# Layer A's output product in paired chunks, and streamed weights released by steps of TensorE

## The chip, the cores and the metric

The kernel runs on one core of a Trainium2 chip, as one launch. A core has TensorE (matrix products; its weight loads are shown apart as PEld), VectorE (DVE), ScalarE (ACT), GpSimd (POOL) and SyncE (SP), each with its own instruction stream, and 16 DMA engines that all of them share. The metric is device time of the launch in microseconds; lower is better. Each kernel is run several times and the median counts. A profiled execution comes beside the runs, and all durations here are from it.

## The reference

Four layers, A B A B, each added to the residual stream of 2048 rows of 640 numbers (bf16). Layer B is linear attention with a softmax feature map, and the change doesn't touch it. Layer A is a recurrence over 64 segments of 32 rows: 8 memory rows and the segment's 32 rows go through attention with 32 heads of 192, and the first 8 output rows are the next segment's memory.

```python
for s in range(n_seg):                                  # 64 segments
    xs = x[:, s * seg_len:(s + 1) * seg_len, :]
    h = jnp.concatenate([mem, xs], axis=1)              # 8 + 32 rows of 640
    q = jnp.einsum('btd,dhe->bhte', h, Wq)              # 32 heads x 192
    k = jnp.einsum('btd,dhe->bhte', h, Wk)
    v = jnp.einsum('btd,dhe->bhte', h, Wv)
    scores = jnp.einsum('bhqe,bhke->bhqk', q, k) * scale
    p = _softmax(jnp.where(mask[None, None], scores, -1e9), axis=-1)
    o = jnp.einsum('bhqk,bhke->bhqe', p, v)
    o = jnp.einsum('bhte,hed->btd', o, Wo)              # the output product
    mem = o[:, :M, :]                                   # feeds the next segment
    outs.append(o[:, M:, :])
```

So a segment can't begin before the memory rows of the one before are there.

## The kernel before, in words

**Segments and rounds.** `A_pre` works out what doesn't depend on the recurrence (the last eight rows of each segment), and `A_chain` runs the 64 segments. In a segment 32 rows (8 of memory, 24 of the input) are worked on in four rounds of eight heads. `order = rounds(s)` is 0, 1, 2, 3 in even segments and 3, 2, 1, 0 in odd ones, so that the weights of the round that ended one segment are there when the next begins. The order of work on every engine is that of the program text (`manual_schedule`), SP's queue of transfers included.

**The projections.** `project(hT, ps, m, n, s, steps)` (L976 to L994) is the product of the segment's 32 rows with one round's weights of Q, K or V: five steps over the 640 inputs, each with four matmuls of 384 columns that write four groups of 32 partitions side by side. `to_raw` (ScalarE, L1001) takes Q and K out of PSUM, `to_rows` (VectorE, L1006 to L1011) turns them, and `v_rows` (ScalarE L1020, VectorE L1022) takes out V. Round n + 1's Q, K and V projections stand between the parts of round n: scores (`scores`, L1028 and L1033), exponential (`weigh`, L1103), values (`attend`, L1044 and L1051), scaling (`scaled`, L1064 and L1066), turning (`turn`, L1167 and L1174).

**The output product.** `wo_round(W, r, OT, first, last, part)` (L1082 to L1088) is one round's share of the output product. It has twelve chunks i, each a 128 x 32 block of attended values (`OT`) against 128 x 640 of output weights. The 640 outputs are spread over four groups of 32 partitions, 160 columns each: 4 matmuls a chunk, 48 a round, 192 a segment, all into one PSUM bank `W`. The round 0 part runs after Q of round 2, parts of round 1 after Q of round 3 and after the loop, round 2 around the last `attend`, and round 3 at the segment's end.

**The end of a segment.** After the last product, one matmul and one weight load keep TensorE from idling (`keep_busy`, `fill(SEG_FILL)`). VectorE turns `W` (L1235) and copies the eight memory rows into `hT` (L1236), input rows 2 to 4 first, then 0 and 1, in the order in which Q of the next segment reads them. Then come `keep_tail` (L1068 to L1075: a reciprocal on VectorE, a scaled copy `otr` on ScalarE, a transposition `otb` on VectorE), `store_tail` (a transfer on POOL's queue) and `keep_rows` (L952 to L955: four ScalarE copies of 32 x 160 out of `W`). The next segment's Q0, K0, V0 and Q1 follow on TensorE, then its first scores.

**Streamed weights.** The weights don't all fit on chip. Of each of Q, K and V, three pieces (of five) of the two end rounds 0 and 3 share slots, and so do the output weights of rounds 0 and 3 (`wo_end`). Each segment therefore loads three pieces of Q, three of V (384 KB each), three of K (in halves of 192 KB) and six of output weights (320 KB): about 5.5 MB, all on SP's queue. A slot's load (`load_slot`) is issued inside `project` of round 0, behind the matmuls that last read the slot. The output weights are issued all six at once (`load_wo`, L1183) after the round 0 product in iteration n = 1. Their readers are round 3's projections and product.

**Fillers.** `FILL` and `SEG_FILL` put single weight loads into TensorE's stream: 65 or 79 after Q0 of a layer's first segment, one at the end of each segment.

Of the kernel before, what the change touches and what calls it, by code (L numbers as in the profile page):

```python
# [117 lines left out]
class Kernel:  # L118
# [523 lines left out]
    def layer_A(self, xn_dram, at_dram, li, x_raw=None):  # L642
# [29 lines left out]
        assert at + 36 * 1280 == ARENA  # L672
        unread = set(res)

        def load_slot(m, r, b, whole=False):
            if holds.get((m, b)) != r:
                holds[m, b] = r
                w = PW if whole or m in "QV" else PW // 2
                for h in range(0, PW, w):
                    nc.sync.dma_start(out=slot[m, b][:, h:h + w], in_=wview[m][:, b, PW * r + h:PW * r + h + w])  # L680

        def load_matrix(m, r):
            for b in range(KC):
# [6 lines left out]
        early = {(0, 4), (0, 5), (2, 4), (2, 5), (1, 0), (1, 1), (1, 2), (1, 3)}  # L690

        def load_wo(r, into=None, part=range(6)):
            t = into if into is not None else wo_end[:, :] if r in (0, 3) else wo_mid[:, 7680 * (r - 1):7680 * r]
            for k in part:
                tk = t[:, 1280 * k:1280 * k + 1280]
                load = nc.sync.dma_start(out=tk, in_=self.wo_rows[r, :, 1280 * k:1280 * k + 1280])
                if r in (0, 3):
                    self.last_load = load

        def piece(m, r, b):  # L700
            assert (m, r, b) in res or holds[m, b] == r
# [217 lines left out]
    def A_chain(self, xn_dram, at_dram, li, load_slot, piece, load_wo, late_wo, wo_mid, wo_end, low):  # L919
# [3 lines left out]
        with tc.tile_pool(name=f"A{li}_ch", reuse_waits="tile", bufs=1) as sp, \  # L923
# [26 lines left out]
                return sp.tile([P, KC, 32], BF16, name="hT", tag="hT")  # L950

            def keep_rows(W):  # L952
                for g in range(4):
                    last = nc.scalar.activation(out=orow[:, 160 * g:160 * g + 160], in_=W[32 * g:32 * g + 32, 0:160], func=ACT.Copy)  # L954
                self.chain_end.append(last)  # L955

            def store_rows(s):
                nc.gpsimd.dma_start(out=at_dram[32 * s:32 * s + 24, :], in_=orow[8:32, :])
# [17 lines left out]
            def project(hT, ps, m, n, s, steps):  # L976
                order = rounds(s)
                r = order[n]
                ns = SLOTS[m]
                for i in steps:  # L980
                    b = (i + KC - ns) % KC if n == 0 else i
                    w = piece(m, r, b)
                    for g in range(4):
                        if m == "V":
                            hp = 2 * (g % 2) + g // 2
                            rhs = w[:, 384 * hp:384 * hp + 384]
                        else:
                            w3 = w[:, 32 * g:32 * g + 32]
                            rhs = ap3(w3, [list(w3.ap[0]), [P, 6], [768, 2], [1, 32]])
                        o = ps  # L990
                        nc.tensor.matmul(o[32 * g:32 * g + 32, 0:384], lhsT=hT[:, b, :], rhs=rhs, start=(i == 0),  # L991
                                         stop=(i == KC - 1), tile_position=(0, 32 * g), skip_group_check=True)
                    if n == 0 and b >= KC - ns:
                        load_slot(m, order[NR - 1], b)  # L994

            def values(hT, n, s, pv, steps):
                project(hT, pv, "V", n, s, steps)
# [26 lines left out]
            def scores():  # L1024

                S = pop.tile([P, 512], F32, name="ps_s", tag="s", bufs=2)
                m = self.mk[0:80, :]
                nc.tensor.matmul(S[0:80, 0:320], lhsT=self.ident[0:80, 0:80], rhs=ap3(m, [list(m.ap[0]), [0, 4], [1, 80]]),  # L1028
                                 start=True, stop=False, skip_group_check=True)
                for x in range(2):  # L1030
                    for i, q0, q1 in ((0, 0, 1), (1, 1, 3), (2, 3, 4)):
                        c0 = 160 * x + (80 if i == 2 else 0)
                        nc.tensor.matmul(S[0:80, c0:c0 + 80 * (q1 - q0)], lhsT=KT[:, 3 * x + i, :], rhs=QT[:, x, q0:q1, :],  # L1033
                                         start=False, stop=(x == 1 and i == 2), skip_group_check=True)
                return S

            pair = [None]

            def attend(E, n):
                O = pop.tile([P, 512], F32, name="ps_o", tag="o0")  # L1040
                V = Vs[n % 2]
                for G in range(2):
                    for h in range(4):
                        nc.tensor.matmul(O[32 * h:32 * h + 32, VH * G:VH * G + 193], lhsT=E[0:80, 80 * h + 32 * G:80 * h + 32 * G + 32],  # L1044
                                         rhs=V[0:80, VH * h:VH * h + 193], start=True, stop=True, tile_position=(0, 32 * h),
                                         skip_group_check=True)
                if n % 2 == 0:
                    pair[0] = pop.tile([P, 512], F32, name="ps_t", tag="o1")
                q, m = (48, 32) if n % 2 == 0 else (64, 16)
                for h in range(4):  # L1050
                    nc.tensor.matmul(pair[0][32 * h:32 * h + m, 0:193], lhsT=E[0:80, 80 * h + q:80 * h + q + m],  # L1051
                                     rhs=V[0:80, VH * h:VH * h + 193], start=True, stop=True, tile_position=(0, 32 * h),
                                     skip_group_check=True)
                return O

# [9 lines left out]
                else:  # L1065
                    nc.vector.tensor_scalar(out=out, in0=i, scalar1=rc[:, G:G + 1], scalar2=None, op0=ALU.mult)  # L1066

            def keep_tail():  # L1068
                rc = sp.tile([P, 1], F32, name="rct", tag="rct")
                nc.vector.reciprocal(out=rc[:], in_=pair[0][:, 192:193])  # L1070
                rows = sp.tile([P, 192], BF16, name="otr", tag="rawk")
                nc.scalar.activation(out=rows[:], in_=pair[0][:, 0:192], func=ACT.Copy, scale=rc[:])  # L1072
                otb = sp.tile([P, 192], BF16, name="otb", tag="otb")
                self.chain_end = [nc.vector.transpose(out=otb[:], in_=rows[:])]  # L1074
                return otb  # L1075

            def store_tail(otb, s, r):
# [4 lines left out]
            def wo_round(W, r, OT, first, last, part=range(12)):  # L1082
                w = low[:, 0:7680] if last_wo == r else wo_end[:, :] if r in (0, 3) else wo_mid[:, 7680 * (r - 1):7680 * r]
                for i in part:
                    for g in range(4):
                        nc.tensor.matmul(W[32 * g:32 * g + 32, 0:160], lhsT=OT[i // 6][:, i % 6 // 2, 32 * (i % 2):32 * (i % 2) + 32],  # L1086
                                         rhs=w[:, 640 * i + 160 * g:640 * i + 160 * g + 160], start=(first and i == 0),
                                         stop=(last and i == 11), tile_position=(0, 32 * g), skip_group_check=True)  # L1088

            def keep_busy(ps, w):  # L1090

# [8 lines left out]
            def weigh():  # L1100
                S = scores()
                E = sp.tile([P, 320], BF16, name="E", tag="E")
                nc.scalar.activation(out=E[0:80, 0:320], in_=S[0:80, 0:320], func=ACT.Exp, scale=scale)  # L1103
                return E

# [23 lines left out]
            for s in range(NSEG):  # L1129
# [5 lines left out]

                def q_or_k(m, n):
                    ps = pqp.tile([P, 512], F32, name="ps_qk", tag="qk")
                    project(hT, ps, m, n, s, range(KC))
                    return to_raw(ps, "rawk" if m == "K" else "raw")

                def v_banks():
# [35 lines left out]
                    load_wo(order[L], low[:, 0:7680])  # L1177
                for n in range(L):
                    raw = q_or_k("Q", n + 1)
                    if n == 1:  # L1180
                        wo_round(W, order[0], OTs[0], True, False)
                        if s < NSEG - 1:
                            load_wo(order[L])  # L1183
                        else:
                            tails = [self.fetch_tails(tb, low) for tb in range(2)]
                    elif n == 2:
                        wo_round(W, order[1], OTs[1], False, False, range(6))
                        otb = keep_tail()
                    E = weigh()
                    to_rows(raw, "Q")  # L1190
                    next_kq(s, n)
                    if n == 2:
                        store_tail(otb, s, order[1])
                    raw = q_or_k("K", n + 1)
                    O = attend(E, n)
                    tails_after(n)
                    rc = weigh_rows(O)
                    to_rows(raw, "K")
                    pv = v_banks()
                    project(hT, pv, "V", n + 1, s, range(KC))  # L1200
                    osc = sp.tile([P, 384], BF16, name="osc", tag="raw")
                    for G in range(2):
                        scaled(osc[:, 192 * G:192 * G + 192], O, rc, G, "s")
# [26 lines left out]
                keep_busy(idle, 512)  # L1230
                fill(SEG_FILL)
                if s + 1 < NSEG:
                    wt = sp.tile([P, KC, 32], F32, name="wt", tag="raw")
                    for b0, b1 in ((2, 5), (0, 2)):
                        nc.vector.transpose(out=wt[:, b0:b1, :], in_=W[:, 0:160].rearrange("p (j b) -> p b j", b=KC)[:, b0:b1, :])  # L1235
                        nc.vector.tensor_copy(out=hT[:, b0:b1, 0:8], in_=wt[:, b0:b1, 0:8])  # L1236
                store_tail(keep_tail(), s, order[L])
                keep_rows(W)
            store_rows(NSEG - 1)

    def fetch_tails(self, tb, low):
# [82 lines left out]
```

## Time and profile before

| what | value |
|---|---|
| median of 3 runs | 3756.55 us (3747.55 to 3760.22) |
| profiled execution | 3738.2 us, its span 3736.4 us |
| granted TensorE clock, mean | 0.956 |
| busy: PE, PEld, DVE, ACT, POOL | 88%, 58%, 63%, 49%, 39% |
| TensorE matmuls recorded | 70,850 |
| transferred | 929.28 MB, mean 249 GB/s |
| chain that ended last, by engine | PE 63%, DVE 11%, issue 9%, DMA 6%, ACT 6%, POOL 1% |

Times in the profile are microseconds from the span's start, unless marked ns. L1086 is line 1086 of the kernel. A group of instructions reads: line, engine, operation, what it writes and reads, shape, count, then busy time and mean ns of one, then the engine's idle time before them and what ended it. "issue" is time in which the engine waited for nothing that the profile shows. Matmuls are pipelined, so their durations overlap; what one costs is read from start to start. In tables by stretch of time, each engine has its busy us and its instructions, and then come the granted clock, the share of the 16 DMA engines' time and GB/s.

### The profile page before, as it was taken

The page shows a single profiled execution, that of the slowest core. Times are in us where ns is not written, and L with a number is a line of the kernel's source. Part 1 is how long each engine was busy: PE and PEld are TensorE (multiplying, and loading weights), DVE is VectorE, ACT ScalarE, POOL GpSimd, SP SyncE. Part 2 cuts the span into 40 slices and gives each one's busy share as a digit, 9 for nine tenths or more (in the row PEclk, how much of TensorE's full clock was granted, in tenths as well). Part 3 has the DMA queues.
Part 4 walks back from the last instruction along what each step waited for, and adds up shares of the span by engine and source line. Part 5 has one row for each costly group of instructions (what it writes and reads, how often), then busy time and mean ns, then how long its engine had stood idle before and what let it go on. Part 6 is the DMA issues. An engine that isn't in the chain of part 4 may idle for free.

```text
span 3736.4 us, 167117 instructions
## 1 busy us (share of the span) xinstructions
PE 3281.7 (88%) x70850; PEld 2159.8 (58%) x71122; DVE 2357.5 (63%) x6591; ACT 1846.2 (49%) x4481; POOL 1454.6 (39%) x3917
## 2 busy tenths in 40 slices
PE   9878888888888888899999888888888888888999
PEld 7655555555555555555377555555555555555553
DVE  5456666666676666646643666666666666666475
ACT  3244555455555555446433455545555555555463
POOL 3344444444444444431122444444444444444310
PEclk9989999899999999999999899989999999999999
DMA  8887887777787877760475787777777877777600
GB/s 319 323 285 260 280 280 274 253 270 266 271 293 271 290 281 267 258 239 9 141 275 207 275 280 275 270 259 259 263 276 270 284 265 269 276 273 273 235 4 29
DMA packets 444966, 929.28 MB, mean 249 GB/s; under 512 B 71722, under 2 KB 203450, under 8 KB 441146
## 3 DMA queue, kind: packets, MB, share of 16 engines
q1 hardware_dynamic: 382746, 821.50, 61.8%
q0 software_dynamic: 59552, 83.85, 7.2%
q8 instruction: 557, 9.13, 1.0%
q10 hardware_dynamic: 1920, 13.24, 0.9%
q14 instruction: 191, 1.56, 0.1%
HBM read 850.47 MB, written 75.69 MB: 248 GB/s over the span
## 4 chain that ended last, share of the span: by engine, by line
PE 63%; DVE 11%; issue 9%; DMA 6%; ACT 6%; POOL 1%; ACTq 0%; SPq 0%; DVEq 0%; POOLq 0%
PE ps_qk L991 20%; PE ps_w L1086 13%; PE ps_v L991 8%; PE ps_s L1033 4%; PE ps_pre L878 3%; DMA arena<-wo_rows 3%; PE ps_s L1028 2%; PE ps_o L1044 2%; ACT Vp L954 2%; PE kv L1279 2%; PE ps_pre L905 2%; ACT osc L1064 2%; DVE KT L1006 2%; ACT raw L1001 1%; DVE osc L1066 1%
## 5 line engine op out<-in xcount | busy, mean ns | idle before, releaser
L991 PE MATMUL ps_qk<-arena,hT 128*32 128x384 bf16 x20480 | 1056.2, 339 | 52.7 <-DVE hT L1236 39.2
L991 PEld LDWEIGHTS <-hT 128*32 128x32 bf16 x30720 | 782.9, 98 | 483.5 <-issue 109.3
L1001 ACT ACTIVATE raw<-ps_qk 128x384 bf16<-128x384 f32 x1024 | 491.9, 491 | 365.1 <-PE ps_qk L991 327.1
L1086 PE MATMUL ps_w<-arena,OT 128*32 128x160 bf16 x18432 | 500.0, 236 | 155.0 <-issue 146.8
L1086 PEld LDWEIGHTS <-OT 128*32 128x32 bf16 x18432 | 358.1, 97 | 285.0 <-issue 176.3
L991 PE MATMUL ps_v<-arena,hT 128*32 128x384 bf16 x10240 | 512.9, 328 | 11.2 <-DMA arena<-in_A_Wv_dram 11.1
L1064 ACT ACTIVATE osc<-ps_o,rc 128x192 bf16<-128x192 f32 x896 | 335.3, 418 | 314.6 <-DVE rc L1058 313.1
L1009 DVE STREAM_TRANSPOSE QT<-raw 128x256 bf16<-128x256 bf16 x512 | 222.6, 435 | 354.0 <-ACT raw L1001 183.2
L967 POOL COPY QT<-kqb 128x64 bf16<-128x64 bf16 x512 | 121.3, 237 | 788.6 <-PE ps_s L1033 726.7
L962 POOL DMA_DIRECT2D kqb<-kqb x512 | 291.7, 570 | 165.3 <-POOL KT L970 146.8
L1103 ACT ACTIVATE E<-ps_s 80x320 bf16<-80x320 f32 x512 | 220.7, 431 | 241.4 <-PE ps_s L1033 237.6
L1006 DVE STREAM_TRANSPOSE KT<-raw 128x384 bf16<-128x384 bf16 x512 | 296.3, 579 | 65.5 <-ACT raw L1001 55.0
L1072 ACT ACTIVATE otr<-ps_t,rct 128x192 bf16<-128x192 f32 x256 | 107.8, 421 | 436.4 <-DVE rct L1070 422.7
L1022 DVE CAST Vp<-ps_v 64x384 bf16<-64x384 f32 x512 | 286.3, 559 | 35.9 <-ACT Vp L1020 20.5
L974 POOL DMA_DIRECT2D Vp<-vb x512 | 259.9, 508 | 101.9 <-PE ps_t L1051 88.0
L1086 PE MATMUL ps_w<-arena,KT 128*32 128x160 bf16 x6144 | 175.2, 278 | 128.3 <-DVE KT L1174 125.4
L1033 PE MATMUL ps_s<-QT,KT 128*80 128x80 bf16 (+1 forms) x3072 | 233.7, 213 | 49.0 <-DVE KT L1006 41.8
L1020 ACT ACTIVATE Vp<-ps_v 64x384 bf16<-64x384 f32 x512 | 246.9, 482 | 26.4 <-PE ps_v L991 25.7
L1033 PEld LDWEIGHTS <-KT 128*80 128x80 bf16 x3072 | 199.0, 119 | 87.9 <-issue 73.8
L1078 POOL DMA_DIRECT2D otb<-otb x256 | 144.5, 565 | 248.7 <-DVE otb L1074 243.1
L1086 PEld LDWEIGHTS <-KT 128*32 128x32 bf16 x6144 | 140.5, 116 | 158.0 <-DVE KT L1174 152.8
L878 PEld LDWEIGHTS <-arena 128*128 128x128 bf16 x1920 | 189.5, 99 | 43.6 <-issue 11.5
(154 smaller groups left out, 4987.1 us busy)
## 6 DMA issues: line engine op xcount, KB each, us to landing
arena<-wo_rows SPq DMA_DIRECT2D x804, 320.0 KB, 7.5
arena<-in_A_Wq_dram SPq DMA_DIRECT2D x427, 384.0 KB, 4.7
arena<-in_A_Wv_dram SPq DMA_DIRECT2D x427, 384.0 KB, 6.3
arena<-in_A_Wk_dram SPq DMA_DIRECT2D x768, 192.0 KB, 4.3
kqb<-kqb POOLq DMA_DIRECT2D x512, 48.0 KB, 5.3
arena<-in_A_Wk_dram SPq DMA_DIRECT2D x43, 384.0 KB, 7.8
vb<-arena POOLq DMA_DIRECT2D x128, 97.0 KB, 6.1
Vp<-vb POOLq DMA_DIRECT2D x512, 24.2 KB, 5.1
```

The costliest lines, as they stand in the source:

```text
L878: nc.tensor.matmul(ps[:, T * i:T * i + T], lhsT=w[b][:, P * c:P * c + P], rhs=xBT[:, b, :], start=(b == 0), stop=(b == KC - 1))
L962: nc.gpsimd.dma_start(out=kqb[:], in_=self.kqb_d[r, :, s, :])
L974: nc.gpsimd.dma_start(out=Vs[n % 2][64:80, :], in_=self.vb_d[s, r].rearrange("g t f -> (g t) f"))
L991: nc.tensor.matmul(o[32 * g:32 * g + 32, 0:384], lhsT=hT[:, b, :], rhs=rhs, start=(i == 0), stop=(i == KC - 1), tile_position=(0, 32 * g), ...
L1001: nc.scalar.activation(out=raw[:], in_=ps[:, 0:384], func=ACT.Copy)
L1006: nc.vector.transpose(out=KT[:, :, 0:64], in_=raw[:, :].rearrange("p (c j) -> p c j", j=64))
L1009: nc.vector.transpose(out=QT[:, :, 0:4:3, 0:64], in_=rv[:, :, 0:3:2, :])
L1020: nc.scalar.activation(out=o, in_=i, func=ACT.Copy)
L1022: nc.vector.tensor_copy(out=o, in_=i)
L1033: nc.tensor.matmul(S[0:80, c0:c0 + 80 * (q1 - q0)], lhsT=KT[:, 3 * x + i, :], rhs=QT[:, x, q0:q1, :], start=False, stop=(x == 1 and i == 2 ...
L1064: nc.scalar.activation(out=out, in_=i, func=ACT.Copy, scale=rc[:, G:G + 1])
L1086: nc.tensor.matmul(W[32 * g:32 * g + 32, 0:160], lhsT=OT[i // 6][:, i % 6 // 2, 32 * (i % 2):32 * (i % 2) + 32], rhs=w[:, 640 * i + 160 * ...
```

## The change

It has two parts.

**Paired chunks.** A chunk i of the output product is now two matmuls of 320 columns instead of four of 160. Even chunks write partition groups 0 and 1, odd chunks groups 2 and 3. Each group holds two separated blocks of 160 outputs, so `W` has 320 columns instead of 160, and holds two partial sums: even chunks in partitions 0 to 63, odd ones in 64 to 127. A segment has 96 of these matmuls instead of 192, and 832 instructions on TensorE instead of 1024. The two halves are added where they are read. At the segment's end VectorE makes four transpositions instead of two, and four additions in place of two copies. In `keep_rows` two ScalarE copies of 64 x 160 bring the upper half to SBUF, and four VectorE additions make the rows. `keep_rows` now stands ahead of `keep_tail`, and `keep_tail` uses another buffer (`OTh`) at the segment's end.

**Released loads.** The three V loads and the six output-weight loads of a segment are put into a list `held`. `release(step, n)` issues the next n of them with a wait on the TensorE instruction `step` added to what they already wait for. The first V load waits for the K projection of round 1, the second for V of round 1, the third for Q of round 2; the six output pieces wait for V of round 2, Q of round 3, the third scores, K of round 3, the third `attend`, V of round 3. The order of transfers on SP's queue stays.

```diff
+        held = []
+        def release(step, n=1):
+            for f in held[:n]:
+                for load in f():
+                    tc.add_manual_dep(load.ins, step.ins.name,
+                                      mybir.DependencyInfo(mybir.DependencyClass.Sync, mybir.DependencyReason.DATA),
+                                      reason="few streamed weights under way")
+            del held[:n]
...
             def keep_rows(W):
-                for g in range(4):
-                    last = nc.scalar.activation(out=orow[:, 160 * g:160 * g + 160], in_=W[32 * g:32 * g + 32, 0:160], func=ACT.Copy)
-                self.chain_end.append(last)
+                tmp = [sp.tile([P, 160], F32, name=f"wh{a}", tag=tag) for a, tag in enumerate(("E", "rawk"))]
+                for a in range(2):
+                    last = nc.scalar.activation(out=tmp[a][64:P, :], in_=W[64:P, 160 * a:160 * a + 160], func=ACT.Copy)
+                    for g in range(2):
+                        c = 320 * a + 160 * g
+                        nc.vector.tensor_tensor(out=orow[:, c:c + 160], in0=W[32 * g:32 * g + 32, 160 * a:160 * a + 160],
+                                                in1=tmp[a][64 + 32 * g:96 + 32 * g, :], op=ALU.add)
+                self.chain_end = [last]
...
                     if n == 0 and b >= KC - ns:
-                        load_slot(m, order[NR - 1], b)
+                        if m == "V":
+                            self.held.append(lambda b=b: load_slot(m, order[NR - 1], b))
+                        else:
+                            load_slot(m, order[NR - 1], b)
...
                 for i in part:
-                    for g in range(4):
-                        nc.tensor.matmul(W[32 * g:32 * g + 32, 0:160], lhsT=OT[i // 6][:, i % 6 // 2, 32 * (i % 2):32 * (i % 2) + 32],
-                                         rhs=w[:, 640 * i + 160 * g:640 * i + 160 * g + 160], start=(first and i == 0),
-                                         stop=(last and i == 11), tile_position=(0, 32 * g), skip_group_check=True)
+                    for g in range(2):
+                        q = 32 * (2 * (i % 2) + g)
+                        rhs = w[:, 640 * i:640 * i + 640].rearrange("p (a g f) -> p a g f", a=2, g=2)[:, :, g, :]
+                        nc.tensor.matmul(W[q:q + 32, 0:320], lhsT=OT[i // 6][:, i % 6 // 2, 32 * (i % 2):32 * (i % 2) + 32],
+                                         rhs=rhs, start=(first and i < 2), stop=(last and i > 9), tile_position=(0, q),
+                                         skip_group_check=True)
...
                     raw = q_or_k("Q", n + 1)
+                    if n > 0:
+                        self.release(self.step)
                     if n == 1:
                         wo_round(W, order[0], OTs[0], True, False)
                         if s < NSEG - 1:
-                            load_wo(order[L])
+                            self.held.extend(lambda k=k: load_wo(order[L], part=[k]) for k in range(6))
...
                     E = weigh()
+                    if n == 2:
+                        self.release(self.scored)
...
                     raw = q_or_k("K", n + 1)
+                    if n != 1:
+                        self.release(self.step)
                     O = attend(E, n)
+                    if n == 2:
+                        self.release(self.attended)
...
-                    project(hT, pv, "V", n + 1, s, range(KC))
+                    self.release(project(hT, pv, "V", n + 1, s, range(KC)))
+                    if n == L - 1 and self.held:
+                        self.release(self.attended, len(self.held))
...
                 if s + 1 < NSEG:
-                    wt = sp.tile([P, KC, 32], F32, name="wt", tag="raw")
+                    wt = [sp.tile([P, KC, 32], F32, name=f"wt{a}", tag=tag) for a, tag in enumerate(("raw", "rawk"))]
                     for b0, b1 in ((2, 5), (0, 2)):
-                        nc.vector.transpose(out=wt[:, b0:b1, :], in_=W[:, 0:160].rearrange("p (j b) -> p b j", b=KC)[:, b0:b1, :])
-                        nc.vector.tensor_copy(out=hT[:, b0:b1, 0:8], in_=wt[:, b0:b1, 0:8])
-                store_tail(keep_tail(), s, order[L])
+                        for a in range(2):
+                            nc.vector.transpose(out=wt[a][:, b0:b1, :],
+                                                in_=W[:, 160 * a:160 * a + 160].rearrange("p (j b) -> p b j", b=KC)[:, b0:b1, :])
+                        for a in range(2):
+                            nc.vector.tensor_tensor(out=hT[64 * a:64 * a + 64, b0:b1, 0:8], in0=wt[a][0:64, b0:b1, 0:8],
+                                                    in1=wt[a][64:P, b0:b1, 0:8], op=ALU.add)
                 keep_rows(W)
+                store_tail(keep_tail("OTh"), s, order[L])
```

`project` returns its last matmul, `scores` and `attend` keep theirs in `self.scored` and `self.attended`, and the load functions return the transfers they issue. In the last segment only the three V loads are held.

More of the change, by code (lines that the diff above doesn't have):

```diff
@@ L673, in layer_A @@
         unread = set(res)
+        held = []
[6 more added lines that the diff above has]
+            del held[:n]
+        self.held, self.release = held, release
         def load_slot(m, r, b, whole=False):
+            loads = []
             if holds.get((m, b)) != r:
@@ L679, in load_slot @@
                 for h in range(0, PW, w):
-                    nc.sync.dma_start(out=slot[m, b][:, h:h + w], in_=wview[m][:, b, PW * r + h:PW * r + h + w])
+                    loads.append(nc.sync.dma_start(out=slot[m, b][:, h:h + w], in_=wview[m][:, b, PW * r + h:PW * r + h + w]))
+            return loads
         def load_matrix(m, r):
@@ L692, in load_wo @@
         def load_wo(r, into=None, part=range(6)):
+            loads = []
             t = into if into is not None else wo_end[:, :] if r in (0, 3) else wo_mid[:, 7680 * (r - 1):7680 * r]
@@ L696, in load_wo @@
                 load = nc.sync.dma_start(out=tk, in_=self.wo_rows[r, :, 1280 * k:1280 * k + 1280])
+                loads.append(load)
                 if r in (0, 3):
                     self.last_load = load
+            return loads
         def piece(m, r, b):
@@ L990, in project @@
                         o = ps
-                        nc.tensor.matmul(o[32 * g:32 * g + 32, 0:384], lhsT=hT[:, b, :], rhs=rhs, start=(i == 0),
+                        last = nc.tensor.matmul(o[32 * g:32 * g + 32, 0:384], lhsT=hT[:, b, :], rhs=rhs, start=(i == 0),
                                          stop=(i == KC - 1), tile_position=(0, 32 * g), skip_group_check=True)
                     if n == 0 and b >= KC - ns:
-                        load_slot(m, order[NR - 1], b)
+                        if m == "V":
+                            self.held.append(lambda b=b: load_slot(m, order[NR - 1], b))
+                        else:
+                            load_slot(m, order[NR - 1], b)
+                return last
             def values(hT, n, s, pv, steps):
@@ L1032, in scores @@
                         c0 = 160 * x + (80 if i == 2 else 0)
[L1033 removed]
+                        self.scored = nc.tensor.matmul(S[0:80, c0:c0 + 80 * (q1 - q0)], lhsT=KT[:, 3 * x + i, :], rhs=QT[:, x, q0:q1, :],
                                          start=False, stop=(x == 1 and i == 2), skip_group_check=True)
@@ L1050, in attend @@
                 for h in range(4):
-                    nc.tensor.matmul(pair[0][32 * h:32 * h + m, 0:193], lhsT=E[0:80, 80 * h + q:80 * h + q + m],
+                    self.attended = nc.tensor.matmul(pair[0][32 * h:32 * h + m, 0:193], lhsT=E[0:80, 80 * h + q:80 * h + q + m],
                                      rhs=V[0:80, VH * h:VH * h + 193], start=True, stop=True, tile_position=(0, 32 * h),
@@ L1066, in scaled, with keep_tail @@
                     nc.vector.tensor_scalar(out=out, in0=i, scalar1=rc[:, G:G + 1], scalar2=None, op0=ALU.mult)
-            def keep_tail():
+            def keep_tail(tag):
                 rc = sp.tile([P, 1], F32, name="rct", tag="rct")
                 nc.vector.reciprocal(out=rc[:], in_=pair[0][:, 192:193])
-                rows = sp.tile([P, 192], BF16, name="otr", tag="rawk")
+                rows = sp.tile([P, 192], BF16, name="otr", tag=tag)
                 nc.scalar.activation(out=rows[:], in_=pair[0][:, 0:192], func=ACT.Copy, scale=rc[:])
                 otb = sp.tile([P, 192], BF16, name="otb", tag="otb")
-                self.chain_end = [nc.vector.transpose(out=otb[:], in_=rows[:])]
+                self.chain_end.append(nc.vector.transpose(out=otb[:], in_=rows[:]))
                 return otb
@@ L1137, in q_or_k @@
                     ps = pqp.tile([P, 512], F32, name="ps_qk", tag="qk")
-                    project(hT, ps, m, n, s, range(KC))
+                    self.step = project(hT, ps, m, n, s, range(KC))
                     return to_raw(ps, "rawk" if m == "K" else "raw")
@@ L1187, in A_chain @@
                         wo_round(W, order[1], OTs[1], False, False, range(6))
-                        otb = keep_tail()
+                        self.chain_end = []
+                        otb = keep_tail("rawk")
                     E = weigh()
+                    if n == 2:
+                        self.release(self.scored)
                     to_rows(raw, "Q")
```

## The prediction

> **What bounds the kernel now.** I read the shares first, then the segments, then one segment's TensorE timeline. TensorE's matmuls are busy 88% of the span, and lie on the chain of waits for 63% of it. Between the first and last of a layer's closing `keep_busy` matmuls lie 1390.8 us (216.0 to 1606.8) and 1409.4 us (2074.8 to 3484.2): layer A's 2 x 63 segment periods are 2800 us of the 3736.4. Only they are touched. From the start times of all matmuls, I cut these periods at fixed matmul numbers within a segment (0 to 508). The mean period is 22.24 us, the shortest 20.65.
>
> ```profile
> q8 instruction: 557, 9.13, 1.0%
> ...
> L1086 PE MATMUL ps_w<-arena,OT 128*32 128x160 bf16 x18432 | 500.0, 236 | 155.0 <-issue 146.8
> ```
>
> The second line (matmul groups) is the output product. 155 us of TensorE's idle time stands before it, and 146.8 of that waits for nothing that the profile shows. One segment's matmuls show where (start, us, instruction, count, idle before):
>
> ```profile
> 1248.77 0.45 PE L1086 MATMUL ps_w<-arena,OT 128*32 128x160 bf16 x16
> 1249.15 0.33 PE L1028 MATMUL ps_s<-mask_st,ident 80*80 80x320 bf16 x1
> 1249.50 0.45 PE L1033 MATMUL ps_s<-QT,KT 128*80 128x80 bf16 x6
> 1249.89 0.61 PE L1086 MATMUL ps_w<-arena,OT 128*32 128x160 bf16 x14
> 1251.39 0.52 PE L1086 MATMUL ps_w<-arena,OT 128*32 128x160 bf16 x18 [0.90 <-issue]
> ```
>
> Fourteen matmuls of one round run, then eighteen of the same kind after a hole, with weights long in place. In all segments the hole is before matmul 406: mean 1.41 us, median 1.59, least 0. Before matmul 279 there is a smaller one (mean 0.17). 406 - 279 is 127 matmuls, with their weight loads 254 instructions. The first fence's instruction queue gives the reason: 557 packets of 16384 bytes for TensorE's 142,629 records, so one packet per 256 instructions, four per segment. The hole is **late code**. Packet times confirm it: where a hole exists, the block is usable 2.53 us after its packet starts (2.39 to 2.66 for eight in ten). How soon that packet starts after the preceding block is entered depends on the weights in flight (bytes issued by SP less bytes moved): 1.25 us (median) with 0.06 MB in flight (matmul 406), 1.92 with 1.38 MB (151), 3.78 with 1.95 MB (279). So after 279 the next block takes 3.78 + 2.53 = 6.3 us, while its instructions last 4.44 (2.22 + 2.22) to 4.8 us. Difference 1.5 to 1.9; seen 1.59. The transfers really fill the engines there and are idle later (last columns: granted clock, DMA share, GB/s):
>
> ```profile
> 1246.00:1248.00 2.00, 2.00 (x67) 1.41 (x59) 1.39 (x5) 1.31 (x4) 0.85 (x4) 1.00 1.03 395
> ...
> 1252.00:1254.00 2.00, 0.99 (x57) 0.79 (x50) 1.29 (x5) 0.42 (x1) 1.31 (x3) 1.00 0.17 51
> ```
>
> The segment's end is another serial stretch (same segment, whole timeline):
>
> ```profile
> 1253.60 1.01 PE L1086 MATMUL ps_w<-arena,KT 128*32 128x160 bf16 x48 [1.01 <-DVE KT L1174]
> ...
> 1254.67 0.28 DVE L1235 STREAM_TRANSPOSE wt<-ps_w 128x96 f32<-128x96 f32 x1
> ...
> 1254.98 0.18 DVE L1236 CAST hT<-wt 128x24 bf16<-128x24 f32 x1
> ...
> 1255.43 0.16 DVE L1070 RECIPROCAL rct<-ps_t 128x1 f32<-128x1 f32 x1
> ...
> 1255.69 0.42 ACT L1072 ACTIVATE otr<-ps_t,rct 128x192 bf16<-128x192 f32 x1 [2.87 <-DVE rct L1070]
> 1256.13 1.21 ACT L954 ACTIVATE Vp<-ps_w 32x160 bf16<-32x160 f32 x4
> ...
> 1257.37 0.87 ACT L1001 ACTIVATE raw<-ps_qk 128x384 bf16<-128x384 f32 x2
> ...
> 1257.89 0.45 DVE L1009 STREAM_TRANSPOSE QT<-raw 128x256 bf16<-128x256 bf16 x1 [1.37 <-ACT raw L1001]
> ...
> 1258.89 0.58 DVE L1006 STREAM_TRANSPOSE KT<-raw 128x384 bf16<-128x384 bf16 x1
> ...
> 1259.62 0.45 PE L1033 MATMUL ps_s<-QT,KT 128*80 128x80 bf16 x6 [0.45 <-DVE KT L1006]
> ```
>
> From the product's end (1254.65) to the scores (1259.62) pass 4.97 us, led by VectorE and ScalarE: the next segment's projections fit inside.
>
> Third, **the clock**. The trace has 69 half-clock stretches, 329 us, all whole multiples of 3.413 us, and most begin at a segment's end. On that grid, a window in which TensorE streams under about 0.41 of the time is followed by half clock (all 36 windows at 0.30 to 0.35, none of 64 at 0.45 to 0.50). The hole helps to make such windows. The cost is seen in the last round, matmuls 460 to 508: mean 1.21 us, 0.84 at full clock.
>
> **The change part by part, per segment.**
>
> (1) Product: 192 matmuls of 160 columns become 96 of 320. 236 ns is no price, since they overlap. Step times of 0.94, 0.52 and 0.38 us for 48, 24 and 16 give 17.5 ns each plus 0.10 per group. A projection's 384 columns cost 38 ns each, so 160 should cost 15.9: columns already set the pace. Between 0 and 96 x 1.6 ns = 0.15 us saved; I take 0.05, near the column end.
>
> (2) Code: 1024 instructions become 832, 3.25 blocks, so the block borders wander by 64 instructions over the segment. In the dense part (matmuls 81 to 460) a block now lasts about 5.2 us: twenty-matmul projections at 0.82, product parts of 0.94 and 0.52, scores 0.55, values 0.25, against 4.8 before. With nine loads released by steps (three V after K1, V1, Q2; six wo after V2, Q3, scores, K3, attend, V3) instead of three and six at once, about 0.3 to 1 MB should be in flight, so 1.3 to 1.9 us + 2.53 = 3.8 to 4.4 us: under 5.2, no hole. Elsewhere a border's block contains the end's waits and is longer. Recovered: 1.41 + 0.17, and 0.04 + 0.07 that stand behind these two (279 to 337, 406 to 424) = 1.69; I take 1.6. The lower bound is 0.6 (a rival below).
>
> (3) Clock: without the hole, the thinnest 3.41 us window at the end holds 0.84 (last round), 0.21 (idle matmul) and some 0.42 of Q0: 0.43, just above 0.41. Recoverable 1.21 - 0.84 = 0.37; between 0 and 0.37 I take 0.25.
>
> (4) Tail. `W` now has two halves to add. To `hT`: two transposes of 0.28 (the second may start 0.08 before the first ends, as neighbouring rows do), two additions of 0.18 (row: the 0.18 copy): ready 0.92 instead of 0.52 us after `W`; then the other half, two of 0.23 and two of 0.17. `keep_rows` now stands ahead of `keep_tail`: four VectorE additions of 160 columns, not in the trace; nearest is the 128x140 `TENSOR_TENSOR` of L438 at 293 ns, and 500 columns there take 656, so 1.01 ns a column: 0.31 each. The reciprocal `rct`, on VectorE behind them, starts at 2.7 instead of 0.78: +1.92. What waits for it is ScalarE's `otr`, and in line behind that `raw` of Q0, QT, KT and the scores. But the four ScalarE copies (1.23 us) between `otr` and `raw` are gone; two copies of 0.29 run during the additions. Net +0.69; I take 0.65. Bounds: 0.15 if all additions overlap their neighbours by 0.08, 1.1 if each costs 0.42 (the 192-column row of L1066) and the small ones 0.23. Projections stay hidden: Q0 starts 0.4 later and still ends before `raw` can be read. On POOL, `store_tail` waits 1.8 us longer; behind it is only `store_rows` and the next copies, due after the scores. Cover gone, each us here is 126 us.
>
> (5) Waits on SP: each held load waits at SP's head, and behind it stand only the other held loads and then the next segment's Q loads, not due before Q0. The last wo piece is released after V3 (about 14.9 us into the segment) and used at 19.2: 4.3 us for 320 KB. Median landing today is 7.5 us in the deep queue; 160 KB in a quiet one (`arena<-attn`) 2.3. With one or two pieces ahead (0.82 us each by packet times) it lands in 3 to 4. Cost 0 to 3.2; I take 0.1. V pieces have over 5 us.
>
> Sum: -0.05 - 1.6 - 0.25 + 0.65 + 0.1 = -1.15 us; x 126 = -145 us. The profiled execution took 3738.2 us (span 3736.4), 18 below the runs' median 3756.55; the change is put on the median: **3612 us**. Its own range, each term at a plausible end, is 3530 to 3730.
>
> A rule of the skill speaks against (2). The Trainium skill, "Runtime: NRT & Kernel Launch", section "Instruction fetch mechanics", says code streams in blocks of 256 instructions, TensorE holding 2048, with the crossing mostly hidden. The block size agrees (557 packets); "hidden" does not (1.41 us). By it, fewer instructions would recover nothing.
>
> **The rivals.** (A) *The fetch stays late*: the 3.78 us comes from the engines being full, not from depth. The dense stretch lasts 12.5 us; a block lies wholly in it if entered in its first 7.3, which of a segment of 21.1 us (22.24 - 1.15) with 3.25 borders are 1.1. Each waits 6.3 - 5.2 = 1.1 us: recovered 1.69 - 1.2 = 0.5, clock 0.1; with the tail nothing is left: 3757. For: 151 and 279 both see engines full. Against: yet they differ, 1.92 and 3.78, with the bytes in flight.
> (B) *The hole isn't late code and stays*: only the tail moves, +0.65 x 126 = 82: 3839. The rule just named points this way. Against: the 254 instructions between holes and the packet times.
> (C) *Late output weights*: the last round waits on its sixth piece, slower than before once that lands later than 4.3 + 1.15 = 5.45 us after release. At 6.3 us (V's median today) it costs 2.0 us x 125 = 250: 3862. For: 7.5 today. Against: pacing is what shortens the queue.
> (D) *Tail at its upper bound* with half the clock gain: -145 + 57 + 16 = -72: 3685, still faster.
>
> **How the numbers follow.** Forecast 0.62, D 0.13, A 0.10, C 0.09, B 0.06. A measurement tells 0.3%, 11 us, from no change. Faster: 0.62 + 0.13 + a few of A = 0.76; same: most of A, 0.07; slower: B, C and the rest of A, 0.17. The range, 3530 to 3762, holds forecast and D and reaches A.
>
> **What would show it.** In the profile after: the instruction queue at about 461 packets (557 - 128 x 0.75); product groups whose idle "issue" falls from 147 us to under 30; fewer half-clock stretches than 69; product end to scores 5.5 to 5.8 us, with four `TENSOR_TENSOR` of 0.3 us ahead of `rct`; wo landing under 5 us. Wrong it is if "issue" holes merely move to other lines, if the last round waits on `wo_rows`, or if the stretch from `W` to the scores exceeds 6.1 us.

## The result, and the profile after

The changed kernel takes **3909.32 us** (median of 4 runs, 3887.2 to 3917.44) against 3757.05 for the one before (3756.55 with the three runs that were there at first): ratio **1.0394**, 95% interval 1.0349 to 1.044. It is slower, where 3612 us were forecast. The profiled execution's span is 3914.7 us against 3736.4, its mean granted clock 0.919 against 0.956.

From the page of the changed kernel: a queue's packets, megabytes and share; the chain's shares; an issue's count, size and median us to landing. The last line is the same issue in the kernel before.

```profile
q8 instruction: 461, 7.55, 0.7%
...
PE 60%; DMA 22%; DVE 8%; issue 5%; ACT 2%; PEld 2%; POOL 1%; SPq 0%; ACTq 0%; DVEq 0%; POOLq 0%
...
arena<-wo_rows SPq DMA_DIRECT2D x804, 320.0 KB, 4.6
...
arena<-wo_rows SPq DMA_DIRECT2D x804, 320.0 KB, 7.5
```

The code is 461 blocks, as forecast. DMA's share of the chain has gone from 6% to 22%, although an output piece now lands 4.6 us after its issue instead of 7.5. The product's groups show both sides (idle time and its releasers stand last; the first line is the last round's group in the kernel before, the other two are the changed kernel's):

```profile
L1086 PE MATMUL ps_w<-arena,KT 128*32 128x160 bf16 x6144 | 175.2, 278 | 128.3 <-DVE KT L1174 125.4 <-DMA arena<-wo_rows 2.7
...
L1115 PE MATMUL ps_w<-arena,OT 128*32 128x320 bf16 x9216 | 459.3, 303 | 7.7 <-DMA arena<-wo_rows 5.0 <-DVE OT L1196 0.8 <-DVE OT L1203 0.2
...
L1115 PE MATMUL ps_w<-arena,KT 128*32 128x320 bf16 x3072 | 185.5, 321 | 288.8 <-DVE KT L1203 171.1 <-DMA arena<-wo_rows 115.9
```

In rounds 0 to 2 the 146.8 us of "issue" are gone: the hole before matmul 406 is no longer there. In the last round (the line that reads `KT`) the idle time went from 128.3 to 288.8 us, and 115.9 of it waits for output weights, against 2.7 before (nearly all the rest of the growth is the wait for `KT`, 125.4 to 171.1). One segment of the changed kernel, TensorE's timeline:

```profile
1183.87 0.88 PE L1115 MATMUL ps_w<-arena,OT 128*32 128x320 bf16 x16
1184.58 0.52 PE L1071 MATMUL ps_o<-Vp,E 80*32 80x193 bf16 x8
1184.85 0.33 PE L1078 MATMUL ps_t<-Vp,E 80*16 80x193 bf16 x4
1184.93 0.65 PE L1115 MATMUL ps_w<-arena,OT 128*32 128x320 bf16 x12
1186.95 0.73 PE L1115 MATMUL ps_w<-arena,KT 128*32 128x320 bf16 x16 [1.37 <-DVE KT L1203]
1188.11 0.32 PE L1115 MATMUL ps_w<-arena,KT 128*32 128x320 bf16 x4 [0.42 <-DMA arena<-wo_rows]
1189.07 0.46 PE L1115 MATMUL ps_w<-arena,KT 128*32 128x320 bf16 x4 [0.64 <-DMA arena<-wo_rows]
1189.29 0.63 PE L1121 MATMUL ps_idle<-arena,ident 128*32 128x512 bf16 x1
```

The sixteen matmuls run through without a hole. The last round stops twice, before its fifth and before its sixth piece (four matmuls each). The chain of waits (start, us, what) turns round this point in segment after segment:

```profile
1322.80 0.84 PE ps_v L1014 x20
1323.65 0.02 issue
1323.66 5.75 DMA arena<-wo_rows
1329.41 0.04 issue
1329.45 0.34 PE ps_w L1115 x4
...
1329.82 0.46 DVE wt L1276 x2
...
1331.57 2.18 PE ps_qk L1014 x28
```

V of round 3 ends, that releases the sixth piece, 5.75 us later it is there, four matmuls follow, then the additions, then the next segment. All of V3, values, turning and the earlier chunks now stand beside this transfer, not ahead of it.

Cutting all segments at the same matmuls, before and after (mean us, 124 neighbouring pairs), gives the account:

| stretch | before | after | |
|---|---|---|---|
| Q3 to third scores (holds matmul 279) | 1.50 | 1.33 | -0.17 |
| rest of round 1, first half of round 2, to last `attend` (holds 406) | 2.10 | 0.75 | -1.35 |
| fourth scores; last `attend`; from it to the last round | 0.65; 0.26; 1.66 | 0.75; 0.35; 2.01 | +0.54 |
| last round | 1.21 | 2.19 | +0.98 |
| from the idle matmul to the next Q0 | 0.79 | 1.19 | +0.40 |
| Q0 to first scores | 4.52 | 5.59 | +1.07 |
| whole period | 22.24 | 23.64 | +1.40 |

The stretches that the table leaves out give -0.07 together. 1.40 x 126 = 176 us, of the 178 us between the two spans. Half-clock time per segment rose from 2.12 to 4.53 us.

### The profile page after: what moved, and what is told of

It is laid out like the page before. It is cut to its first block, busy times and chain, and to the rows that moved or that the text cites. A ratio compares the mean times of both kernels' runs of the same rounds, so it can differ in the third digit from the quotient of the medians.

```text
span 3914.7 us, 143255 instructions
## 1 busy us (share of the span) xinstructions
PE 3417.4 (87%) x58528; PEld 2006.4 (51%) x58834; DVE 2627.7 (67%) x7607; ACT 1767.4 (45%) x4225; POOL 1446.4 (37%) x3917
## 4 chain that ended last, share of the span: by engine, by line
PE 60%; DMA 22%; DVE 8%; issue 5%; ACT 2%; PEld 2%; POOL 1%; SPq 0%; ACTq 0%; DVEq 0%; POOLq 0%
PE ps_qk L1014 23%; DMA arena<-wo_rows 19%; PE ps_v L1014 11%; PE ps_w L1115 6%; PE ps_s L1060 3%; PE ps_pre L896 3%; PE ps_s L1055 2%; DVE wt L1276 2%; PE ps_o L1071 2%; PE ps_pre L923 1%; DVE hT L1279 1%; PEld L896 1%; DMA arena<-otb 1%; PE kv L1323 1%; PE ps_pq L463 1%
## 5 line engine op out<-in xcount | busy, mean ns | idle before, releaser
L1014 PE MATMUL ps_qk<-arena,hT 128*32 128x384 bf16 x20480 | 1155.1, 365 | 106.4 <-DVE hT L1279 84.6
L1014 PEld LDWEIGHTS <-hT 128*32 128x32 bf16 x30720 | 829.9, 105 | 634.0 <-issue 206.0
L1014 PE MATMUL ps_v<-arena,hT 128*32 128x384 bf16 x10240 | 566.4, 353 | 15.7 <-DMA arena<-in_A_Wv_dram 15.7
L1115 PE MATMUL ps_w<-arena,OT 128*32 128x320 bf16 x9216 | 459.3, 303 | 7.7 <-DMA arena<-wo_rows 5.0
L1115 PE MATMUL ps_w<-arena,KT 128*32 128x320 bf16 x3072 | 185.5, 321 | 288.8 <-DVE KT L1203 171.1
L973 ACT ACTIVATE wh<-ps_w 64x160 f32<-64x160 f32 x256 | 76.6, 299 | 674.6 <-DVE wt L1276 423.8
L1115 PEld LDWEIGHTS <-OT 128*32 128x32 bf16 x9216 | 222.3, 96 | 153.2 <-DVE OT L1196 74.7
L1115 PEld LDWEIGHTS <-KT 128*32 128x32 bf16 x3072 | 82.2, 96 | 398.0 <-DVE KT L1203 214.7
L1276 DVE STREAM_TRANSPOSE wt<-ps_w 128x96 f32<-128x96 f32 x504 | 104.4, 245 | 190.0 <-PE ps_w L1115 186.0
```

The costliest lines, as they stand in the source:

```text
L1014: last = nc.tensor.matmul(o[32 * g:32 * g + 32, 0:384], lhsT=hT[:, b, :], rhs=rhs, start=(i == 0), stop=(i == KC - 1), tile_position=(0, 3 ...
L1115: nc.tensor.matmul(W[q:q + 32, 0:320], lhsT=OT[i // 6][:, i % 6 // 2, 32 * (i % 2):32 * (i % 2) + 32], rhs=rhs, start=(first and i < 2), s ...
```

## The experiments

Medians of the kernel before differ between the groups of runs (3757, 3729, 3726 and 3741 us), so each ratio is against the kernel before on the same chip. My theory after the result: the released output pieces come too late, and the waits set off half clock; a second cost is the longer tail. The rival: the paired chunks' tail is all of it.

**Each part alone.** Nothing held; and product and tail of before, with released loads:

```diff
-                        if m == "V":
-                            self.held.append(lambda b=b: load_slot(m, order[NR - 1], b))
-                        else:
-                            load_slot(m, order[NR - 1], b)
+                        load_slot(m, order[NR - 1], b)
...
-                            self.held.extend(lambda k=k: load_wo(order[L], part=[k]) for k in range(6))
+                            load_wo(order[L])
```

> Paired chunks alone: the V and output-weight loads are issued as in the kernel before, nothing is held. Theory (the released output pieces land too late, and the wait in the last round puts the next segment at half clock): the 1.29 us a segment that the last round waits for pieces goes to under 0.1, and some of the half clock with it; some code holes come back (0.7 us a segment). About 3909 - 126 x 1.0 = 3785 us (3730 to 3840). Rival (the pieces cost nothing, the longer tail of the paired chunks is the whole loss): only the holes come back, 3909 + 88 = about 4000 us.

Measured: 3745.43 us, ratio 1.0065 (1.0034 to 1.0095). No waits for pieces (0.01 us a segment), last round 0.88 us, half clock 0.73 us a segment. The code holes are nearly gone without any released load: TensorE's idle time on "issue" within the segments is 18 us in all, against 151 in the kernel before and 1 in the change, where some 0.7 us a segment (88 us) were expected back. The stretch that held the hole still takes 1.07 us (0.75 in the change), for another reason, the wait of `attend` for `Vp`:

```profile
L1068 PE MATMUL ps_o<-Vp,E 80*32 80x193 bf16 x4096 | 186.1, 249 | 48.7 <-DMA Vp<-vb 43.1 <-issue 4.3
```

This is the 24 KB transfer on POOL's queue that brings the extra V rows; the change has 5.2 us of this wait. What is left beside it is the tail: Q0 to scores 5.26, idle matmul to Q0 1.16. The theory's range holds the time.

> Released loads alone: output product, tail and keep_rows are those of the kernel before. Theory (late pieces): the last round waits about 1.2 us a segment for pieces, the code hole of 1.41 us before matmul 406 is gone, 0.4 us of it are given back to VectorE's queue: 3757 + 126 x (1.29 + 0.42 + 0.4 - 1.6) = about 3820 us (3760 to 3870). Rival (the tail is the whole loss): the hole is gone and nothing is lost, 3757 - 126 x 1.2 = about 3606 us.

For this one `wo_round`, `keep_tail`, `keep_rows` and the end of the segment are those of the kernel before. Measured: 3783.11 us, ratio 1.0187 (1.0122 to 1.0253), in the theory's range, far from the rival's 3606. Its group of the last round:

```profile
L1108 PE MATMUL ps_w<-arena,KT 128*32 128x160 bf16 x6144 | 175.8, 241 | 307.3 <-DVE KT L1196 167.5 <-DMA arena<-wo_rows 138.9
```

138.9 us of waits for pieces without any paired chunk. And the hole is gone with 1024 instructions: 0.03 us before matmul 406 (1.39 before). The block that follows matmul 278 starts its transfer after 1.00 us (median) with 0.54 MB in flight, against 3.78 us with 1.95 MB. So the two parts cure the same hole, each alone, and each adds a cost of its own.

**Which loads.** Only the V loads released:

```diff
-                            self.held.extend(lambda k=k: load_wo(order[L], part=[k]) for k in range(6))
+                            load_wo(order[L])
```

> The kernel after the change, but the six output-weight loads are issued at once as before; only the three V loads are released by steps. Theory (late pieces): as with paired chunks alone, last round's waits under 0.1 us a segment, 3700 to 3800 us; the holes are smaller than with nothing held, because V is no longer in flight when the output weights are issued. Rival (tail): about 3909 to 4000 us.

3767.08 us, ratio 1.0125 (1.0069 to 1.0181); pieces in time (0.03 us). The idle time on "issue" is smaller, as expected (7.5 us against 18 with nothing held), but the waits for `Vp` grow from 43.1 to 62.6 us, so the stretch takes 1.27 us against 1.07: holding V was no gain. The output pieces earlier:

```diff
                         if s < NSEG - 1:
                             self.held.extend(lambda k=k: load_wo(order[L], part=[k]) for k in range(6))
+                            self.release(self.step)
...
-                    if n == 2:
+                    if n == 1:
                         self.release(self.scored)
...
-                    if n != 1:
+                    if n < 2:
                         self.release(self.step)
                     O = attend(E, n)
-                    if n == 2:
+                    if n == 1:
                         self.release(self.attended)
```

> The kernel after the change, but the six output pieces are released about 3 us earlier: at once behind the round 0 product, then by the second scores, K2, the second attend, V2 and Q3. Theory (late pieces): the last one is released near 13.5 us instead of 16.5 and lands before it is read; waits of the last round under 0.2 us a segment, half clock less: about 3909 - 126 x 1.5 = 3720 us (3680 to 3780). Rival (tail): 3900 us, no change.

3756.51 us, ratio 1.007 (1.0032 to 1.0109): the theory. Its last round:

```profile
L1115 PE MATMUL ps_w<-arena,KT 128*32 128x320 bf16 x3072 | 140.7, 319 | 145.7 <-DVE KT L1203 142.5 <-DMA arena<-wo_rows 2.9
```

115.9 us of waits became 2.9, and the half clock went with them (4.53 to 1.04 us a segment). Per segment 1.30 us less, by moving six issues. The first is now issued 9.0 us into the segment, the last at 12.9, and its packets end at 19.4 (medians); in the change 12.4, 16.3 and 21.7. The landing is longer here (6.4 us), and in time.

**The same release on the kernel before's product.**

> Product and tail of the kernel before (1024 instructions a segment), with the three V loads and the six output pieces released by steps, the pieces about 3 us earlier than in the change. Theory: no waits for pieces in the last round, the hole before matmul 406 about halved, some 0.1 us of it given back to VectorE's queue: 100 us faster than the kernel before, about 3635 us (3600 to 3690). Rival (releasing loads costs by itself): as slow as released loads alone, about 3783 us.

3700.83 us, ratio 0.9941 (0.9906 to 0.9976): faster, but less than expected. The hole is still there:

```profile
L1108 PE MATMUL ps_w<-arena,OT 128*32 128x160 bf16 x18432 | 498.2, 237 | 136.3 <-issue 126.8 <-DMA arena<-wo_rows 4.8 <-DVE OT L1189 2.4
```

With 1.90 MB in flight after matmul 278 the block's transfer starts after 3.56 us, as before. Here early pieces and prompt code exclude each other. With 832 instructions they don't: the run with early pieces above has 9.1 us of "issue" within the segments, and pays for the early pieces with 59.2 us of waits for `Vp` instead.

**The tail.** `keep_rows` without VectorE: four ScalarE copies of 64x160 into one buffer (bf16), four additions on POOL. This rounds the two partial sums of the output rows to bf16 before they are added.

```diff
+                wh = sp.tile([P, 320], BF16, name="wh", tag="E")
+                for a in range(2):
+                    for x in range(2):
+                        last = nc.scalar.activation(out=wh[64 * a:64 * a + 64, 160 * x:160 * x + 160],
+                                                    in_=W[64 * x:64 * x + 64, 160 * a:160 * a + 160], func=ACT.Copy)
...
+                        nc.gpsimd.tensor_tensor(out=orow[:, c:c + 160], in0=wh[q:q + 32, 0:160], in1=wh[q:q + 32, 160:320],
+                                                op=ALU.add)
```

> The run with early pieces, and in it the sums of keep_rows leave VectorE: ScalarE copies both halves (four copies of 64x160) and POOL adds them, behind store_tail's transfer, so no addition stands ahead of the reciprocal. Theory (the four additions and the two copies that wait for each other are the tail's extra time): last product matmul to scores falls from 6.55 to about 5.3 us at full clock, 3757 - 126 x 1.25 = about 3600 us (3570 to 3660). Rival (the stretch is set by the additions for the memory rows and Q0's later start): 6.2 us or more, 3710 us or more.

3736.54 us, ratio 1.0021 (0.9993 to 1.0049): a miss. The time is the rival's, the mechanism is not: last product matmul to scores fell to 5.58 us at full clock, where the rival had 6.2 or more. The tail did shorten (Q0 to scores 5.25 to 4.53 us), but 0.52 us came back between first scores and Q2:

```profile
ACT E L1138 <- POOL Vp L983: 126.9, 99, 4.2
```

(who waits for whom, us, times, longest). The exponential writes the buffer that POOL's sums read, and POOL had first waited for `otb` to send it off.

> Paired chunks alone (no load held), with the sums of keep_rows on POOL as in the run before. Theory (tail): last product matmul to scores from 6.55 to about 5.3 us: 3745 - 157 = about 3590 us (3560 to 3650). Rival: 3700 us or more.

3720.73 us, ratio 0.9977 (0.9953 to 1.0): the same miss, 0.57 us by the same wait (140.1 us). With the sums ahead of `store_tail` in POOL's order:

```diff
                 tmp = keep_rows(W)
-                store_tail(keep_tail("OTh"), s, order[L])
-                add_rows(tmp)
+                otb = keep_tail("OTh")
+                add_rows(tmp)
+                store_tail(otb, s, order[L])
```

> Paired chunks alone with the sums on POOL, and POOL adds them ahead of store_tail's transfer instead of behind it. Theory (in the run before, the first exponential waits for POOL's sums, since they share a buffer and POOL first waits for the late otb): the 0.58 us a segment between the first scores and Q2 go back to zero (2.85 to 2.27), 3721 - 73 = about 3650 us (3620 to 3680). Rival (POOL itself is too slow for these sums, wherever they stand): 3700 us or more.

3670.14 us, ratio 0.9806 (0.9768 to 0.9843).

> Early output pieces with the sums on POOL, ahead of store_tail's transfer. Theory: 0.52 us a segment less than with the sums behind it, 3737 - 65 = about 3670 us (3630 to 3700). Rival (POOL too slow): 3720 us or more.

3667.87 us, ratio 0.9797 (0.9755 to 0.9839). In both, first scores to Q2 is 2.27 us again, and the exponential's waits for POOL's sums are 0.6 us in all in the second.

**A middle release**, on top of that: `scored` also releases at n = 2, `attended` never.

> As the run with the sums on POOL first, but the six output pieces are released between the early times and those of the change: behind the round 0 product, second scores, K2, V2, Q3, third scores (near 14.5 us; 13.5 early, 16.7 in the change). Theory (a late last piece costs, fewer bytes in flight shorten the code hole): pieces still in time (under 0.3 us a segment), hole smaller than the 0.5 us of the early release: 3620 to 3680 us. Rival (lateness starts at any delay): 1 us a segment or more of waits in the last round, 3750 us or more.

**3661.0 us**, ratio **0.9781** (0.9746 to 0.9817), the fastest; its interval overlaps those of the two runs before, so the schedule itself is not shown to matter, nor, with the sums on POOL, that releasing loads gains anything over holding none (3670.14). Pieces wait 8.0 us in all in the last round. It beats both kernels, the one before by about 2%.

**The clock.** Four more idle matmuls ahead of the last round:

```diff
                 idle = pqp.tile([P, 512], F32, name="ps_idle", tag="qk")
+                for _ in range(4):
+                    keep_busy(idle, 512)
+                wo_round(W, order[L], OTs[L], False, True)
```

> The kernel after the change with four more matmuls of the idle kind (512 columns) ahead of the last round, where TensorE waits for KT. Theory (half clock at the segment's start is a cost of its own, set off by the thin windows at the end): half-clock time falls well under 4.5 us a segment and Q0 to scores from 5.59 to 5.25 us; waits for pieces stay; 3909 - 126 x 0.35 = about 3865 us (3840 to 3890). Rival (the clock only slows what waits anyway): 3909 us, within 10.

> The kernel after the change once more, beside the others on the same chip, to set the run with four idle matmuls against it. Theory: half-clock time 4.5 us a segment and Q0 to scores 5.6 us again, about 35 us slower than that run's 3875 us: 3895 to 3920 us. Rival (the idle matmuls changed nothing): 3875 us.

With idle matmuls 3874.82 us, ratio 1.0377 (1.0322 to 1.0431); the change again 3903.17, ratio 1.0428 (1.0384 to 1.0471). Half clock fell from 3.85 (4.53 in the first profile) to 1.70 us a segment, Q0 to scores from 5.45 (5.59) to 5.31, the waits for pieces stayed (some 1.3 us). Both times lie in the theory's ranges, but the two ran on different chips and their intervals overlap, so the price of the half clock, some 0.14 to 0.28 us a segment by the profiles, isn't settled. Other traces differ too: in the change's, Q0 to scores takes 5.25 us in the 24 segments that have no half clock there and 5.68 in the other 102, but with paired chunks alone it is 5.26 either way.

## Why the prediction failed, step by step

**Late loads (5)** is the step that failed: 0.1 us a segment taken, some 1.4 us of holes in the last round measured (0.04 before). A hole is here a step of over 0.3 us between the starts of two matmuls, less the usual 0.07; as idle time the profile gives 115.9 us, 0.92 a segment. The deadline was read rightly (V3's end to the last round 4.2 us). The landing was not. "3 to 4 us" took a nearly quiet queue with one or two pieces ahead. But the six releases are bunched: the first is issued at 12.4 us, the other five by 16.3, while the DMA engines had been busy for only 0.57 and 0.67 of the time in the two microseconds from 12 to 14 us (V was done); in the kernel before they are busy all of that time. When the sixth piece is issued, four others are still on their way (the second lands at 17.3), and it lands after 5.9 us in the median. Packets of pieces also took 124 ns in the mean against 110. Rival (C) had this mechanism, at a chance of 0.09, and its break-even of 5.45 us was passed. Its sum for a landing after 5.9 us would be some 56 us of loss, though, and 152 were measured: the tail and what came back of the code gain are the rest. Moving the releases alone took the waits away, and 3.2% of the time (ratio 1.0394 to 1.007).

**Tail (4)**: the mechanism was right, the size half. From the last product matmul to the scores at full clock, 5.23 us became 6.53: +1.3 for the 0.65 taken. The additions cost 0.32 us each as forecast (0.31). What failed is "two copies of 0.29 run during the additions". The changed kernel's timeline:

```profile
1189.57 0.45 DVE L1276 STREAM_TRANSPOSE wt<-ps_w 128x96 f32<-128x96 f32 x2 [1.66 <-PE ps_w L1115]
...
1190.47 0.38 DVE L1276 STREAM_TRANSPOSE wt<-ps_w 128x64 f32<-128x64 f32 x2
...
1190.97 0.30 ACT L973 ACTIVATE wh<-ps_w 64x160 f32<-64x160 f32 x1 [4.81 <-DVE wt L1276]
...
1191.30 0.65 DVE L976 TENSOR_TENSOR Vp<-ps_w,wh 32x160 bf16<-32x160 f32 x2
...
1191.98 0.30 ACT L973 ACTIVATE wh<-ps_w 64x160 f32<-64x160 f32 x1 [0.72 <-DVE Vp L976]
...
1192.32 0.65 DVE L976 TENSOR_TENSOR Vp<-ps_w,wh 32x160 bf16<-32x160 f32 x2 [0.36 <-ACT wh L973]
...
1192.98 0.17 DVE L1097 RECIPROCAL rct<-ps_t 128x1 f32<-128x1 f32 x1
```

ScalarE's first copy starts only when VectorE has done its last transposition of `W`, the second only behind the first two additions, whose successors then wait for it. Both waits are semaphores that the built program carries (the second copy waits for the one that the second addition raises); whether this order is needed, no run here shows. Copies and additions run in turn, and the reciprocal starts 3.4 us after the product, not 2.7. Taking the additions off VectorE, with POOL in the right order, is worth 75 us without held loads by the medians of two groups of runs (3745 to 3670), 2.6% by their ratios (1.0065 and 0.9806).

**Code (2)**: right. 461 blocks, the holes gone (-1.52 us; 1.6 taken). But the row was read as all gain, and 0.54 us came straight back: the hole had covered other work. In the changed kernel the last `rc` runs directly behind a `CAST` and two `hT` transpositions on VectorE, where before it had waited for TensorE (`rc` waited 137.9 us for it in all, now 11.9); the step before the last round, in which TensorE waits for KT, grew from 1.23 to 1.65 us. And the released loads weren't needed for it: with paired chunks alone "issue" falls from 151 to 18 us. What the Trainium skill's "Runtime: NRT & Kernel Launch", section "Instruction fetch mechanics", calls mostly hidden was a hole of 1.39 us before matmul 406 and 0.03 with the loads released alone; the measurement decides.

**Clock (3)**: not gained. 0.25 us was to come from the last round, where half-clock time did fall (0.68 to 0.45 us a segment); from Q0 to V0 it rose from 0.78 to 3.23. The thinnest windows stood at 0.43 by the prediction, against a threshold of 0.41 read from the trace, and the waits of step 5 make them thinner. Where pieces are in time it came out as forecast (last round 0.94 us with early pieces, 1.21 before).

**Product (1)**: right, nothing gained: 48 matmuls 0.94 us, 24 of double width 0.93.

## What to carry to other kernels

A released load has a deadline. Add up its release, everything still on its way ahead of it, and a landing measured under such a load, before calling it early enough; a shorter landing after issue is no sign that it comes in time. Before counting an idle hole as gain, look at what the other engines finish under it. And where two partial sums must be added on the path that joins two steps, lay the additions out with their buffers and reader order: here an engine off the path made a loss of 0.7% into a gain of 2%.

## What the runs showed of the hardware that was not expected

How soon the packet of TensorE's next code block starts is not told by how busy the DMA engines are: at two borders of the kernel before their time is taken alike (1.04 and 1.02 in the next microsecond), and the medians from border to packet are 1.92 and 3.78 us. Over the borders that the argument rests on it rises with the bytes in flight: 1.00 us at 0.54 MB, 1.92 at 1.38 MB and 3.56 to 3.78 at 1.9 MB. Bytes are not all of it either: with the loads released alone, the border at matmul 406 has 3.0 us at 0.92 MB, and what delays that packet, no run here shows.

A half-clock stretch needs no idle window. On the grid of 3.41 us, count each matmul as streaming until the next one starts, and at most for the time that its columns take at full clock (384 columns some 160 ns, from a projection's twenty matmuls, four side by side, in 0.81 us). Of the windows of the kernel before in which TensorE streamed for 0.30 to 0.35 of the time, all 36 were followed by half clock, of those at 0.45 to 0.50 (some 60) none; the changed kernel's 71 windows at 0.30 to 0.35 all were too.
